# Two tokens to a partition in the first two steps of a gated linear-attention and FFN kernel: batches of a pair in separate halves of the partitions

## Chip, cores and metric

The kernel runs on one core of one Trainium2 chip. The metric is the device time of one execution in microseconds (us). A core has a matrix engine (PE, with a separate row PEld for its weight loads), a vector engine (DVE), an activation engine (ACT), a general engine (POOL), a sync engine (SP) that issues DMAs, and 16 DMA engines that all queues share. PE reads its operands from SBUF (128 partitions) and writes into PSUM (8 banks of 128 partitions by 512 float32).

## What is computed

A recurrence over 768 tokens for 4 batches and 8 heads of width 48, and a feed-forward network on its output:

```python
f = 1.0 / (1.0 + np.exp(-f_logit))
for t in range(S):
    state = f[:, :, t, :, None] * state + np.einsum('bhd,bhe->bhde', k[:, :, t], v[:, :, t])
    y[:, :, t] = np.einsum('bhd,bhde->bhe', q[:, :, t], state)
x = np.ascontiguousarray(attn_out.transpose(0, 2, 1, 3)).reshape(B * S, H * D)
gate = np.maximum(x @ w_gate, 0.0)
out = gate * (x @ w_val) @ w_out          # 3072 x 384 -> 1536 -> 384
```

Inputs and output are float32 in HBM. A token's 48 values of one head are 192 contiguous bytes, and two neighbouring tokens of a head are 384.

## The kernel before

**Steps.** The tokens are cut into six steps (c = 0 to 5) of 128 tokens. A step has four batches, worked on as two pairs (0, 1) and (2, 3). For each pair the kernel loads f, k, q, v (384 KB each, one DMA each). Then, per batch: ACT turns f into log-gates (exp, then ln), PE sums them along the tokens with a triangular matrix, ACT takes the exponentials of plus and minus that sum, and products give scaled k and q ("hats"). They are transposed so that head columns lie on partitions (into qkT). Scores k.q within the step are matmuls of 48 rows, two head parities in two row tiles of the PE array; DVE multiplies them by a causal mask (ptm). "intra" (L759) makes the transposed output y in four column tiles of 128 rows by 32 columns from ptm and v (vpad), and from step 1 on from the state of the step before too; ACT copies y to xT. "state" (L810) makes the new state's sum from hats and vpad.

**Steps 0 to 2 and 3 to 5.** In steps 1 and 2 the hats are transposed on PE (`pe_hats`), from step 3 on by DMA. Step 0 is special (`twos = (0,)`): for f, k and q a partition holds two neighbouring tokens, so that DMA packets are 384 bytes instead of 192; the partition is 2 x (token pair) + (batch of the pair), so that even and odd partitions belong to different batches. Two masks (`upto`, `below`) that keep the batches apart do the summing over tokens, with two matmuls of 384 columns for each of the two tokens i. After the transposes a token order with one batch to a row is restored by strides (`tokens`). v of step 0 is loaded with one token to a partition. The state needs k with one token to a partition too, so `attention_back` (L631 to L637) transposes the hats of k back on PE, four matmuls and one DVE copy for each batch, behind the outputs of step 0.

**FFN.** For each hidden block j of 12, three matmuls for the gate and three for the value (L834; 512 columns, or 256 where half of the batches are taken alone: blocks 0 to 5 of steps 0 to 2, `halves`), a ReLU on ACT (L840), a product on DVE (L844); then 12 matmuls of 384 columns for each batch (L877), a copy on ACT and a store. The last batch of all is split in two (L857).

**Order of the work.** A planner (`Plan`) takes every operation with a cost and a priority, simulates five engine queues, the DMA queue and eight PSUM banks with a limit for each kind of tile, and fixes one order for each engine; waits on semaphores are derived from it. FFN operations have a low priority on PE (P + 1000) and fill what attention leaves. On the chip each engine works through its list in that order, whatever is late.

**Loads.** SP issues f0.0 k0.0 q0.0 v0.0 f0.1 k0.1 q0.1 v0.1 (step.pair), later f1.0 and so on. POOL issues the nine weight loads, which also turn float32 to bfloat16, in thirds: wg0 only after f0.1 has landed, wv0, then wg1 only after q0.1, wv1, wg2, wv2, and wo0 after q1.0. f1.0 is issued only after wv1 has landed. The list is `first` (L319). Until 15 us the plan puts matmuls on zeros (L938) between PE's real work.

Of the kernel before, what the change touches and what calls it, by code (L numbers as in the profile page):

```python
# [299 lines left out]
def bass_hgrn2_outer__then__ffn_reglu_kernel(  # L300
# [10 lines left out]
    twos = (0,)  # L311
    pe_hats = {(1, 0), (1, 1), (2, 0), (2, 1)}
    halves = {0: 6, 1: 6, 2: 6}
    x_way = {(c, pr): "tiled" if c < 3 else "xbar" for c in range(6) for pr in range(2)}
    s_twin = {(c, pr) for c in range(6) for pr in range(2)} - {(0, 0), (1, 0)}
    y_twin = {(1, 1), (2, 0), (2, 1)}
# [57 lines left out]
    pick2 = sb("pick2", [128, 2], BF16)  # L374
    ident = sb("ident", [128, 128], BF16)
# [4 lines left out]
    pl = Plan({"bc": 2, "bc4": 4, "tp": 2, "s": 4, "y": 2, "kv": 1, "f": 4})  # L380
# [28 lines left out]
    def triangle(t, name, base, prio):  # L409
# [9 lines left out]
                                         pattern=[[0, 64], [1, 2]], channel_multiplier=-1), ["pick"], ["pick"], occ=0.3, prio=-20)  # L419
# [10 lines left out]
    add("DVE", lambda: ve.tensor_copy(pick2[:], same.ap[:, 0:2]), [same], ["pick2"], occ=0.1, prio=-19)  # L430
# [30 lines left out]
    def load(n, c, b0, b1, after=()):  # L461
        last = tails.get("load")
        t = ld[n]
        both = c in twos and n != "v"
        if both:
            src = bass.AP(tensor=srcs[n].tensor, offset=b0 * H * S * D + c * C * D,
                          ap=[[2 * D, C // 2], [S * D, 2 * H], [1, 2 * D]])
            dst = bass.AP(tensor=t, offset=slot_of(n, c, b0 // 2) * 2 * HD, ap=[[NL[n] * 2 * HD, 128], [2 * D, H], [1, 2 * D]])
        else:
            src = bass.AP(tensor=srcs[n].tensor, offset=b0 * H * S * D + c * C * D,  # L470
                          ap=[[D, C], [S * D, (b1 - b0) * H], [1, D]])
            dst = t[:, slot_of(n, c, b0 // 2), :, :, :].rearrange("p b h d -> p (b h) d")
        op = add("SP", lambda: sy.dma_start(dst, src), [], in_keys(n, c, b0, b1),  # L473
                 occ=0.7 if both else 1.0, lat=0.9, prio=c * 100, after=after,
                 follows=[last] if last else [])
        tails["load"] = op
        dma(op, f"{n}{slot_of(n, c, b0 // 2)}", 0.95 * (b1 - b0), (64, 19, 27) if both else (128, 13.5, 23))
        return op
# [20 lines left out]
    loads, done = [], {}  # L499
    for item in first:  # L500
        item, _, behind = item.partition("@")
        gate = [done[behind]] if behind else []
        if item[0] == "w":
            op = load_w(item[:2], int(item[2:]), gate)
        else:
            c, pr = (int(x) for x in item[1:].split("."))
            op = load(item[0], c, 2 * pr, 2 * pr + 2, gate)
        done[item] = op
        if item[0] != "w":
            loads.append(op)  # L510

    def chain(line, *args, **kw):

        last = tails.get(line)
        tails[line] = add(*args, follows=[last] if last else [], **kw)
        return tails[line]
# [10 lines left out]
    def tokens(c, b, x, p, lo=0, hi=128):  # L527
        qi = (c * B + b) % NQ
        if c not in twos:
            return qkT[lo:hi, qi, x, p, :]  # L530
        row, two = NQ * 2 * NP * C, b % 2
        return bass.AP(tensor=qkT, offset=lo * row + (qi - two) * 2 * NP * C + x * 2 * NP * C + p * 2 * C + two,
                       ap=[[row, hi - lo], [2, C]])
# [18 lines left out]
    def attention_pair(c, b0):  # L552
# [3 lines left out]
        raw = {n: ld[n][:, slot_of(n, c, pr), :, :, :].rearrange("p b h d -> p (b h d)") for n in "fkq"}  # L556
        by_i = {n: raw[n].rearrange("p (h i d) -> p i h d", h=H, i=2) for n in "fkq"}
        key = {n: in_keys(n, c, b0, b0 + 2) for n in "fkq"}
# [6 lines left out]
            follows=tails.pop("first q", []), **act_t(2 * HD))  # L565
        heads = lambda b_: b_.ap[:, 0:HD].rearrange("p (h d) -> p h d", h=H)
        for i in range(2):
            bc, ek = Bank("bc4"), Bank("bc4")

            def cum(i=i, bc=bc):  # L570
                for o in range(2):
# [3 lines left out]
            ex = expo[:, e0 + i, 0, :]  # L575
            add("ACT", lambda bc=bc, ek=ek: sc.activation(ek.ap[:, 0:HD], bc.ap[:, 0:HD], AF.Exp, scale=1.0),
                [bc], [ek], prio=P + 2 + i, opens=[ek], **act_t(HD))
            eqk = bc if i else f"expq{e0}_0"
            add("ACT", lambda bc=bc, i=i, ex=ex: sc.activation(bc.ap[:, 0:HD] if i else ex, bc.ap[:, 0:HD], AF.Exp, scale=-1.0),
                [bc], [eqk], prio=P + 2 + i, **act_t(HD))  # L580
            e, hi = ("DVE" if i else "POOL"), his[i]
            hk_op = add("DVE", lambda i=i, hi=hi, ek=ek: ve.tensor_tensor(hats[:, hi, 1, :, 0:D], by_i["k"][:, i], heads(ek), ALU.mult),
                        key["k"] + [ek, f"hats{hi}"], hk_(hi), prio=P + 2 + i, **dve_t(HD))
            add(e, lambda e=e, i=i, hi=hi, bc=bc, ex=ex: engine[e].tensor_tensor(
                hats[:, hi, 0, :, 0:D], by_i["q"][:, i], heads(bc) if i else ex.rearrange("p (h d) -> p h d", h=H), ALU.mult),
                key["q"] + [eqk, f"hats{hi}"], hq_(hi), prio=P + 3 + i, follows=[hk_op] if i else [], **elem_t(e, HD))
# [9 lines left out]
        for j in range(2):  # L596
            lo = 64 * j
            add("ACT", lambda lo=lo, j=j: sc.activation(
                dec[ai][lo:lo + 64, b0:b0 + 2, :, j].rearrange("p b n -> p n b"),
                tot.ap[lo:lo + 64, 0:2 * NP].rearrange("p (n b) -> p n b", n=NP), AF.Exp, scale=-1.0),  # L600
                [tot, f"dec{ai}"], [f"dec{ai}_{b}{j}{hh}" for b in (b0, b0 + 1) for hh in range(2)], prio=P + 10, **act_t(8))
        for x in (1, 0):
            tp = Bank("tp")

            def transposes(x=x, tp=tp):
                t16 = tp.ap[:, :].bitcast(BF16)
                for p in range(NP):
                    for i in range(2):
                        mm = te.transpose(t16[:, 2 * C * p:2 * C * (p + 1)].rearrange("q (r i b) -> q r i b", i=2, b=2)[:, :, i, :],
# [5 lines left out]
            e = "DVE" if x else "ACT"  # L615
            op = add(e, (lambda tp=tp, dst=dst: sc.activation(dst, tp.ap[:, :].bitcast(BF16), AF.Copy)) if e == "ACT"  # L616
# [3 lines left out]
            if not x and b0 == 0:  # L620
                tails["first q"] = [op]

    def attention_back(c, b, behind):
        w = c * B + b
        hi, qi = w % NH, w % NQ
        tp = Bank("tp")

        def transposes():
            t16 = tp.ap[:, :].bitcast(BF16)
            for p in range(NP):  # L630
                mm = te.transpose(t16[:, p * C:(p + 1) * C], tokens(c, b, 1, p), ident[:])  # L631
            return mm
        P = w * 10
        tails["transposes"] = add("PE", transposes, ["ident", f"qkT{qi}_10", f"qkT{qi}_11"], [tp], occ=0.3, lat=PE_L, prio=P + 30,
                                  opens=[tp], follows=[behind, tails["transposes"]])
        add("DVE", lambda: ve.tensor_copy(hats[:, hi, 1, :, :].rearrange("p h d -> p (h d)"), tp.ap[:, :].bitcast(BF16)[:, 0:4 * C]),
            [tp], hk_(hi), prio=P + 31, follows=[behind], **dve_t(256))  # L637

    def attention_front(c, b):
# [32 lines left out]
        if c < NC - 1:  # L672
            for j in range(2):
# [9 lines left out]
        add("POOL", lambda: gp.tensor_tensor(hq, qin[:, b % 2, :, :], ex[:, 0, :].rearrange("p (h d) -> p h d", h=H),  # L683
                                             ALU.mult),
            in_keys("q", c, b, b + 1) + [f"expq{ei // 2 * 2}_{ei % 2}", f"hats{hi}"], hq_(hi), prio=P + 2, **pool_t(HD))
# [21 lines left out]
    def attention(c, bs):  # L707
        units = []
        for b in bs:
# [5 lines left out]
                in_keys("v", c, b, b + 1) + [f"vpad{w % NV}"], [f"v_{w % NV}"], prio=w * 10 + (55 if c in twos else 3), **pool_c(HD))  # L715
# [58 lines left out]
        xi, ybank, yop = c % NX, {}, {}  # L774
        tiled = x_way[c, bs[0] // 2] == "tiled"
        for part in ([units] if tiled and (c, bs[0] // 2) in y_twin else [[u] for u in units]):
# [4 lines left out]
            op = chain("intra", "PE", rows, [t for u in part for t in need(u) + ([f"vpad{u[1] % NV}"] if tiled else [])], ys,  # L781
                       occ=(0.34 if c else 0.19) * len(part) + 0.235 if tiled else 0.38, lat=PE_L, prio=part[0][1] * 10 + 7, opens=ys)
            for u, y in zip(part, ys):
                ybank[u[0]], yop[u[0]] = y, op
        for b, w, _ in units:
# [12 lines left out]
            if c in twos:  # L798
                behind.append(yop[b])
                later.append(lambda b=b, w=w: update(c, b, w))  # L800
            elif c < NC - 1:
                update(c, b, w)

    def update(c, b, w):
# [9 lines left out]
        if c in twos:  # L814
            attention_back(c, b, behind[-1])
        chain("state", "PE", state, hk_(hi) + [f"hats{hi}", f"v_{w % NV}"], [kv],
              occ=0.18, lat=PE_L, prio=P + (32 if c in twos else 6), opens=[kv])
        new_state(kv, c, b, w, P + (25 if c in twos else 0))
# [50 lines left out]
    def ffn_out(g, bs, cuts=1):  # L869
# [14 lines left out]
        for b in bs:  # L884
# [5 lines left out]
            both = [(bass.AP(tensor=out.tensor, offset=at, ap=[[DM, C], [1, DM]]), osb[oi][:, :])]  # L890
# [4 lines left out]
    groups = {c: [(0, 2, range(0, n)), (2, 4, range(0, n)), (0, 4, range(n, NJ))] for c, n in halves.items()}  # L895
    pend = []
    for c in range(NC):
# [4 lines left out]
        behind, later = [], []  # L902
        for b in range(0, B, 2):
# [5 lines left out]
            attention(c, (b, b + 1))  # L909
# [24 lines left out]
    order = pl.settle([(bk, warm_until if bk is spare else 0.0) for bk in banks], rounds=8, early=set(done.values()))  # L934
# [94 lines left out]
```

## Time and profile before

| what | value |
|---|---|
| median of three runs (lowest, highest) | 196.01 us (194.18, 196.87) |
| the profiled execution | 195.26 us |
| its span from first to last instruction | 193.5 us |
| PE busy | 184.2 us, 95% |
| ACT, DVE, POOL busy | 111.0, 106.1, 75.9 us |
| granted PE clock | 1.00 |
| DMA packets, data | 118,196; 31.74 MB |
| of them under 512 bytes | 111,136 |
| queue of SP, share of 16 engines' time | 68.1% |
| queue of POOL (weights) | 11.4% |

A time in the tables of the profile is in us from the start of the span. A group of instructions is written by line, engine, operation and tile, with its count, its busy time and the mean of one. "idle before" is the time in which the engine stood still ahead of these instructions, with what released it. The PE's matmuls are pipelined and their recorded ends are modelled, so this document takes the distance from one start to the next as the cost of a matmul group, and not the recorded durations.

### The profile page before, as it was taken

How to read it: one execution, taken by the hardware profiler on the slowest of the kernel's cores; microseconds unless marked ns; L12 is line 12 of the kernel's file. 1: busy time of each engine (PE TensorE's matmuls, PEld its weight loads, DVE VectorE, ACT ScalarE, POOL GpSimd, SP SyncE). 2: the span in 40 equal slices, each digit the busy share in tenths (PEclk: the TensorE clock that was granted, in tenths of full speed). 3: DMA queues.
4: the chain of work that ended last, by engine and by line, in shares of the span. 5: the costliest groups of instructions: out<-in, count | busy, mean ns of one | idle time of the engine just before them, and what ended most of it. 6: DMA issues, size and time to landing. Idle time of an engine off the chain costs nothing.

```text
span 193.5 us, 4448 instructions
## 1 busy us (share of the span) xinstructions
PE 184.2 (95%) x1773; PEld 110.7 (57%) x1790; DVE 106.1 (55%) x195; ACT 111.0 (57%) x250; POOL 75.9 (39%) x108
## 2 busy tenths in 40 slices
PE   6986898999999999999999999999999999999995
PEld 1445694465788556767755544554555555544564
DVE  7756884671668878354776643743635622443300
ACT  3777439763596779838757758377343544244322
POOL 8377002958275949783533471634230000000000
PEclk9999999999999999999999999999999999999999
DMA  4999999999898999999796998998954220111113
GB/s 131 276 283 207 206 201 207 207 199 239 199 244 167 202 201 192 231 193 247 161 192 132 194 207 172 221 226 170 204 87 106 64 61 0 41 41 44 41 43 119
DMA packets 118196, 31.74 MB, mean 164 GB/s; under 512 B 111136, under 2 KB 118176, under 8 KB 118176
## 3 DMA queue, kind: packets, MB, share of 16 engines
q1 hardware_dynamic: 114192, 27.93, 68.1%
q0 software_dynamic: 3984, 3.54, 11.4%
q8 instruction: 14, 0.23, 0.5%
q14 instruction: 6, 0.05, 0.1%
HBM read 25.95 MB, written 4.72 MB: 158 GB/s over the span
## 4 chain that ended last, share of the span: by engine, by line
PE 70%; DMA 16%; SPq 5%; ACT 2%; DVE 2%; POOL 2%; issue 1%
PE ps L834 36%; PE ps L877 23%; DMA q_in<-in_q_dram 6%; DMA wv<-in_moe_w_val_dram 5%; SPq L473 4%; DMA f_in<-in_f_logit_dram 3%; DMA v_in<-in_v_dram 3%; PE ps L724 2%; PE ps L658 2%; PE ps L694 2%; PE ps L759 1%; PE ps L810 1%; DVE ptm L734 1%; PE ps L857 1%; POOL hats L683 1%
## 5 line engine op out<-in xcount | busy, mean ns | idle before, releaser
L844 DVE TENSOR_TENSOR gT<-relu,ps 128x512 bf16<-128x512 bf16 (+1 forms) x90 | 51.2, 578 | 53.9 <-PE ps L834 38.8
L834 PE MATMUL ps<-xT,wv 128*128 128x512 bf16 (+1 forms) x263 | 60.2, 336 | 1.8 <-DMA wv<-in_moe_w_val_dram 1.3
L840 ACT ACTIVATE relu<-ps 128x512 bf16<-128x512 f32 (+1 forms) x90 | 45.3, 511 | 27.6 <-PE ps L834 27.0
L834 PE MATMUL ps<-xT,wg 128*128 128x512 bf16 (+1 forms) x261 | 59.6, 335 | 0.9 <-ACT relu L840 0.5
L877 PE MATMUL ps<-wo,gT 128*128 128x384 bf16 x276 | 49.5, 326 | 0.1
L877 PEld LDWEIGHTS ps<-wo,gT 128*128 128x128 bf16 x276 | 25.9, 98 | 17.2
L834 PEld LDWEIGHTS ps<-xT,wv 128*128 128x128 bf16 x270 | 24.6, 98 | 19.4 <-DMA wv<-in_moe_w_val_dram 1.7
L834 PEld LDWEIGHTS ps<-xT,wg 128*128 128x128 bf16 x270 | 25.2, 98 | 17.9 <-ACT relu L840 0.4
L734 DVE TENSOR_TENSOR ptm<-ps,tri 128x512 bf16<-128x512 f32 x48 | 30.5, 684 | 8.3 <-PE ps L724 8.2
L680 POOL TENSOR_TENSOR hats<-k_in,expo 128x384 bf16<-128x384 f32 x20 | 19.8, 1000 | 20.8 <-ACT expo L668 11.0
L887 ACT ACTIVATE osb<-ps 128x384 f32<-128x384 f32 x23 | 11.2, 489 | 26.1 <-PE ps L877 26.1
L683 POOL TENSOR_TENSOR hats<-q_in,expo 128x384 bf16<-128x384 f32 x20 | 19.8, 1000 | 6.5 <-DMA q_in<-in_q_dram 6.5
L549 POOL TENSOR_TENSOR st<-ssum,dec 128x384 bf16<-128x384 f32 x16 | 13.3, 830 | 15.7 <-DVE ssum L547 15.5
L649 ACT ACTIVATE f_in<-f_in 128x768 f32<-128x768 f32 x10 | 8.4, 843 | 12.1 <-DMA f_in<-in_f_logit_dram 12.1
L714 POOL CAST vpad<-v_in 128x384 bf16<-128x384 f32 x24 | 11.7, 505 | 3.2 <-DMA v_in<-in_v_dram 3.2
L547 DVE TENSOR_TENSOR ssum<-ps,st 128x384 f32<-128x384 f32 x16 | 8.8, 552 | 4.9 <-PE ps L810 4.9
L668 ACT ACTIVATE expo<-ps 128x384 f32<-128x384 f32 x20 | 9.9, 493 | 0.5 <-PE ps L661 0.3
L670 ACT ACTIVATE expo<-ps 128x384 f32<-128x384 f32 x20 | 9.9, 496 | 0.0
L699 DVE COPY qkT<-ps 128x1024 bf16<-128x1024 bf16 x8 | 5.5, 690 | 7.5 <-PE ps L694 7.4
L724 PEld LDWEIGHTS ps<-qkT 48*128 48x128 bf16 x192 | 5.4, 94 | 5.3 <-issue 1.9
L651 ACT ACTIVATE bneg<-f_in 128x768 bf16<-128x768 f32 x10 | 8.4, 836 | 0.0
L724 PE MATMUL ps<-qkT 48*128 48x128 bf16 x192 | 7.6, 217 | 0.6 <-ACT qkT L616 0.5
(76 smaller groups left out, 146.2 us busy)
## 6 DMA issues: line engine op xcount, KB each, us to landing
f_in<-in_f_logit_dram SPq DMA_DIRECT2D x12, 384.0 KB, 5.6
k_in<-in_k_dram SPq DMA_DIRECT2D x12, 384.0 KB, 4.9
q_in<-in_q_dram SPq DMA_DIRECT2D x12, 384.0 KB, 5.7
v_in<-in_v_dram SPq DMA_DIRECT2D x12, 384.0 KB, 5.3
out_dram<-osb SPq DMA_DIRECT2D x23, 192.0 KB, 2.4
wg<-in_moe_w_gate_dram POOLq DMA_DIRECT2D x3, 384.0 KB, 7.7
wv<-in_moe_w_val_dram POOLq DMA_DIRECT2D x3, 384.0 KB, 8.8
wo<-in_moe_w_out_dram POOLq DMA_DIRECT2D x3, 384.0 KB, 6.2
```

The lines of the kernel that those rows point to most:

```text
L549: add("POOL", lambda: gp.tensor_tensor(t4(s_new), t4(tmp), rate, ALU.mult), [key] + dk, [f"S{b}_{c % 2}"], prio=P + 8, **pool_t(HD))
L668: add("ACT", lambda: sc.activation(ex[:, 1, :], bc.ap[:, 0:HD], AF.Exp, scale=1.0), [bc], [f"expk{ei}"], prio=P + 1, **act_t(HD))
L680: add("POOL", lambda: gp.tensor_tensor(hk, kin[:, b % 2, :, :], ex[:, 1, :].rearrange("p (h d) -> p h d", h=H), ALU.mult), in_keys("k", c, ...
L683: add("POOL", lambda: gp.tensor_tensor(hq, qin[:, b % 2, :, :], ex[:, 0, :].rearrange("p (h d) -> p h d", h=H), ALU.mult), in_keys("q", c, ...
L714: add("POOL", lambda vin=vin, vout=vout: gp.tensor_copy(vout, vin.rearrange("p (n j) d -> p n j d", j=2)), in_keys("v", c, b, b + 1) + [f" ...
L724: mm = te.matmul(s[j].ap[:, p * C:(p + 1) * C], tokens(c, b, 1, p, lo, lo + D), tokens(c, b, 0, p, lo, lo + D))
L734: add("DVE", lambda mi=mi, j=j, s=s: ve.tensor_tensor(ptm[mi][:, j, :, :], s.ap[:, :].rearrange("p (n t) -> p n t", n=NP), mask, ALU.mult) ...
L834: mm = te.matmul(bank.ap[:, 0:n], wt[:, kt, j * 128:(j + 1) * 128], xT[xi][:, kt, n0:n1], start=(kt == 0), stop=(kt == NK - 1))
L840: add("ACT", lambda: sc.activation(relu[ri][:, 0:n], gate.ap[:, 0:n], AF.Relu), [gate], [f"relu{ri}"], prio=P, **act_t(n))
L844: add("DVE", lambda: ve.tensor_tensor(gT[gi][:, j, n0:n1], relu[ri][:, 0:n], val.ap[:, 0:n], ALU.mult), [val, f"relu{ri}"], [f"gT{gi}_{j}_ ...
L877: mm = te.matmul(o[b].ap[:, 0:DM], gT[gi][:, j, b * C:(b + 1) * C], wo[:, j, :], start=(j == 0), stop=(j == NJ - 1))
L887: add("ACT", lambda b=b, oi=oi: sc.activation(osb[oi][:, :], o[b].ap[:, 0:DM], AF.Copy), [o[b]], [f"osb{oi}"], prio=P, **act_t(DM))
```

## The change

Steps 0 and 1 (`twos = (0, 1)`) now both work on pairs with two tokens to a partition. The partition is 64 x (batch of the pair) + (token pair): each batch has 64 partitions of its own. v is loaded in the same way. Each of these sixteen loads is now two DMAs, one for each half of the partitions. Transposes need no strides. Scores are matmuls of 48 rows by 64 columns in 64x64 tiles (32 for a pair instead of 16), masked with a new mask `mask2` for each of the two tokens i. Outputs from ptm and v are matmuls in 64x32 tiles (64 for a pair instead of 32), one chain for both batches; in step 1 the part from the old state stays in 128x32 tiles (24 for a pair). States are matmuls in 64x128 tiles, two that add up for each batch and pair of heads (16 for a pair instead of 8). `attention_back` is gone. In step 1 the sums over tokens take two matmuls of 384 columns for each token i, as in step 0, and the scaled q of its first pair are made on DVE instead of POOL. In step 0 the copy of the transposed q moves from ACT to DVE. The PSUM limit of "kv" goes from 1 to 2. The rows of the output stores of steps 0 and 1 are permuted in the address pattern of the store.

```diff
-    twos = (0,)
-    pe_hats = {(1, 0), (1, 1), (2, 0), (2, 1)}
+    twos = (0, 1)
+    pe_hats = {(2, 0), (2, 1)}
...
+    on_dve = {(1, 0, 0, 0), (1, 0, 0, 1)}
...
-    pl = Plan({"bc": 2, "bc4": 4, "tp": 2, "s": 4, "y": 2, "kv": 1, "f": 4})
+    pl = Plan({"bc": 2, "bc4": 4, "tp": 2, "s": 4, "y": 2, "kv": 2, "f": 4})
...
+    for i, src, name in ((0, upto, "upto"), (1, below, "below"), (1, upto, "upto")):
+        lo = [m for m in range(2) if not (i and (name == "upto") != (m == 1))]
+        add("POOL", lambda i=i, src=src, lo=lo: gp.tensor_tensor(
+            mask2[:, i, lo[0]:lo[-1] + 1, :], src[:, 0:64].unsqueeze(1).to_broadcast([128, len(lo), 64]),
+            src[:, 64:128].unsqueeze(1).to_broadcast([128, len(lo), 64]), ALU.add), [name], [f"mask2_{i}{m}" for m in lo],
+            prio=-9, **pool_t(64 * len(lo)))
...
-        both = c in twos and n != "v"
+        both, one = c in twos, b1 - b0 == 1
         if both:
-            src = bass.AP(tensor=srcs[n].tensor, offset=b0 * H * S * D + c * C * D,
-                          ap=[[2 * D, C // 2], [S * D, 2 * H], [1, 2 * D]])
-            dst = bass.AP(tensor=t, offset=slot_of(n, c, b0 // 2) * 2 * HD, ap=[[NL[n] * 2 * HD, 128], [2 * D, H], [1, 2 * D]])
+            row = NL[n] * 2 * HD
+            moves = [(bass.AP(tensor=t, offset=64 * i * row + slot_of(n, c, b0 // 2) * 2 * HD, ap=[[row, 64], [2 * D, H], [1, 2 * D]]),
+                      bass.AP(tensor=srcs[n].tensor, offset=(b0 + i) * H * S * D + c * C * D,
+                              ap=[[2 * D, C // 2], [S * D, H], [1, 2 * D]])) for i in range(2)]
...
-    def attention_back(c, b, behind):
...
+        def scores(its):
+            for i in its:
+                for p in range(NP):
+                    for j in range(2):
+                        for b in range(2):
+                            mm = te.matmul(s[i][j].ap[64 * b:64 * b + 64, p * C:(p + 1) * C],
+                                           tokens(c, b0 + b, 1, p, 64 * j, 64 * j + D, i), tokens(c, b0 + b, 0, p, 64 * j, 64 * j + D))
...
+            for i in range(2):
+                for at, (n, p, col, j) in enumerate(todo):
+                    lo = 32 * (n % 4)
+                    for b in range(2):
+                        mm = te.matmul(y[b].ap[lo:lo + 32, n // 4 * C:(n // 4 + 1) * C],
+                                       vpad[vs[i]][64 * b:64 * b + 64, col:col + 32], ptm[ms[i]][64 * b:64 * b + 64, j, p, :],
+                                       start=(first and i == 0 and at < 4), stop=(i == 1 and at >= 12), skip_group_check=True)
...
+            def state():
+                for p in range(NP):
+                    for i in range(2):
+                        for b in range(2):
+                            mm = te.matmul(kv[b].ap[:, p * 96:(p + 1) * 96],
+                                           hats[64 * b:64 * b + 64, his[i], 1, 2 * p:2 * p + 2, :].rearrange("p h d -> p (h d)"),
+                                           bass.AP(tensor=vpad[vs[i]], offset=64 * b * VW + p * VSTEP, ap=[[VW, 64], [64, 2], [1, D]]),
+                                           start=(i == 0), stop=(i == 1), skip_group_check=True)
```

## The prediction

> **What bounds the kernel now.** I read the page first: PE is busy 95%. The PE timeline says since when. The first FFN matmul is at 16.58; two waits on weights follow and one on ACT, and from 31 to 66 us PE stands still for no more than 0.2 us at a time:
>
> ```profile
> 16.58 0.49 PE L834 MATMUL ps<-xT,wg 128*128 128x256 bf16 x3
> ...
> 18.12 0.50 PE L834 MATMUL ps<-xT,wv 128*128 128x256 bf16 x3 [0.60 <-DMA wv<-in_moe_w_val_dram]
> ...
> 22.67 0.50 PE L834 MATMUL ps<-xT,wv 128*128 128x256 bf16 x3 [0.71 <-DMA wv<-in_moe_w_val_dram]
> ...
> 30.27 0.60 PE L834 MATMUL ps<-xT,wg 128*128 128x512 bf16 x2 [0.50 <-ACT relu L840]
> ```
>
> The number after the start is the length; brackets give the idle time and its releaser. The third wait is a ReLU behind the exp of f1.0, which waits for its load at the head of ACT's queue. Later gaps come to 2 us in all. So the end is: arrival of the weights, plus PE's work after it. The POOL timeline shows what sets the weights:
>
> ```profile
> 10.68 0.96 POOL L493 DMA_DIRECT2D wg<-in_moe_w_gate_dram  x1 [0.79 <-DMA f_in<-in_f_logit_dram]
> 11.63 0.78 POOL L493 DMA_DIRECT2D wv<-in_moe_w_val_dram  x1
> 13.06 0.77 POOL L493 DMA_DIRECT2D wg<-in_moe_w_gate_dram  x1 [0.64 <-DMA q_in<-in_q_dram]
> ```
>
> The weights wait for f0.1 and q0.1, and these for what lies ahead in SP's queue. The page's second part shows the DMA engines full from there on, with two rates:
>
> ```profile
> DMA  4999999999898999999796998998954220111113
> GB/s 131 276 283 207 206 201 207 207 199 239 199 244 167 202 201 192 231 193 247 161 192 132 194 207 172 221 226 170 204 87 106 64 61 0 41 41 44 41 43 119
> ```
>
> A slice is 4.84 us: loads run at some 280 GB/s, weights alone at 206. Counted in the trace's packets: 864 packets of 384 bytes in the best microsecond (18.5 ns each on one of 16 engines), 1,335 of 192 bytes (12.0 ns). A load of 384 KB is thus 64 packets an engine, 1.2 us, or 128 packets, 1.5 us. First packet at 2.34; f0.1 has landed at 10.03, q0.1 at 12.46, wg0 15.86, wv0 17.77, wv1 22.30, a third every 1.9 us.
>
> **What the Trainium skill says.** "SBUF — State Buffer", Door 1: The DMA port swizzle: 64 partitions reach only 8 of the 16 ports, 196 GB/s measured for 1 MiB against 328 with 128 partitions, and two DMAs to the two halves ran only 6% faster than one. The kernel before has no such load, so nothing here shows it; its loads span all partitions at 280. "DMA: Bandwidth & Descriptors", Queues, rings and completion order: engines switch between queues by packets of several descriptors. The trace agrees that weights hold SP's queue back: from 35 to 36 us 198 weight packets went and 27 of SP's, though SP had loads queued. "TensorEngine Tiling (Array Packing)", Key Properties: tiles work side by side, a change of mode drains the array. The trace agrees: sixteen scores take 51.43 to 51.99 = 0.56, where two tiles side by side give 16 x 28.3 ns = 0.45, so 0.1 for the drains.
>
> **PE's work, part by part.** From the timeline, start to start:
>
> ```profile
> 55.86 0.35 PE L759 MATMUL ps<-qkT,st 128*32 128x128 bf16 x12
> 56.04 0.40 PE L759 MATMUL ps<-ptm,vpad 128*32 128x128 bf16 x16
> 56.26 0.34 PE L759 MATMUL ps<-qkT,st 128*32 128x128 bf16 x12
> 56.43 0.40 PE L759 MATMUL ps<-ptm,vpad 128*32 128x128 bf16 x16
> 56.76 0.50 PE L834 MATMUL ps<-xT,wv 128*128 128x256 bf16 x3
> ```
>
> 56 matmuls in 0.90: 14.2 ns each (four tiles, 56.6 ns per 128 columns) and 0.1.
>
> Step 1 before: sums 0.53 a pair (38.98 to 39.51), scores 0.56 and 2 x 0.33, outputs 0.90 and 2 x 0.51, states 4 x 0.17. Together 1.06 + 1.22 + 1.92 + 0.68 = 4.9 us; transposes are the same before and after. After, a pair: sums 4 x 0.165 (L572, 12.94 to 13.60) + totals 0.20 (eight L592, 7.17 to 7.37) = 0.86; scores 32 in four tiles, 32 x 14.2 ns + 0.1 = 0.55; outputs 24 x 14.2 ns + 64 x 7.1 ns + 0.15 = 0.95 if eight tiles overlap; states 16 of 96 columns (42.5 ns alone, two side by side), between 0.34 and 0.68 plus 0.1, I take 0.5. Twice that: 5.7. Step 1 costs +0.8.
>
> Step 0 after the wait at 22.67: `attention_back` goes, 0.68 + 0.22 (L631) = -0.9; states +0.3. Scores and outputs of its second pair lie ahead of that wait and are covered (+0.1 if not). Sum for PE: +0.2. Bounds: that eight tiles issue fast enough is not shown; the trace has weight load and matmul of one tile starting 3.5 ns after those of the last, eight make 28 ns, within 56.6, so I take the overlap. If only four overlapped: +0.45 for each pair of step 1, +0.9.
>
> **The ramp.** Each load becomes two DMAs. SP's issue of one load takes 0.65 to 0.74 (1.61 and 0.81 in its timeline), the shortest issue of any 0.33; two halves of 0.4 stay below a load's transfer. v0.0 and v0.1 get 384-byte packets. If ports don't matter: 1.2 instead of 1.5, twice; f0.1 lands 0.3 to 0.5 earlier. If each half is held to 8 ports: an engine writes 384 bytes in 18.5 ns; by the 218 GB/s that the skill states for 8 ports (an estimate from "SBUF — State Buffer", Door 1) it is 384 x 16 / 218 = 28.2 ns, 1.8 us a load. Between lies this: the sixteen landings of one load in the trace are spread over 0.34 to 0.5 us and half a load lasts 0.6, so engines that share a port are partly out of step. I take 25 ns, 1.6 us. Then f0.1 has landed at 2.34 + 5 x 1.6 + 0.35 = 10.7 (+0.65), q0.1 at 13.9 (+1.4), still ahead of the first weight data (13.5 + 0.65 = 14.2), so wg1 follows without a hole. v0.1 now ends beside the weights and costs them some 0.5. wv1: +1.1, and PE with it.
>
> Of the rest ahead of the weights: the q copy leaves ACT (1.0 us at 11.15, in front of ln f0.1) for DVE at about 10.65, so the first scores come 0.8 earlier than 12.21; outputs then wait for all four masks, not two, and xT is ready at 16.2, as now (16.25). Covered by wv0; without that cover it would be worth 0.3 either way. The v casts on POOL (8.94) stand ahead of wg0's issue; v0.0 lands at 9.1, casts end by 10.1, before f0.1. mask2's three small POOL operations fall into its idle time from 4.6 to 8.0. Off PE the rest moves work that is not the bound: DVE loses four copies of 0.42 and gains two products of 0.55 and the two copies of 0.69; POOL loses two products of 1.0.
>
> **New waits in step 1.** Transposes, scores, outputs and states now wait for a whole pair. In the kernel before, the outputs of step 1's second pair come at 55.86 and its xT is used from about 57.4, little slack; q1.1 lands at 46.09. Step 1's loads take 1.6 instead of 1.5, no gain. The head-of-queue wait at 30.27 moves along with wv1. I put 0.3 on this, from -0.7 (that wait gone) to +1.5.
>
> **Sum.** 1.1 (weights) + 0.2 (PE) + 0.3 = +1.6 us: the profiled execution 195.26 (span 193.5 and 1.8 around it) becomes 196.9; the median of the runs shown stands 0.75 above it, 197.6.
>
> **Rivals.** (1) Ports don't matter. For: the halves alternate in one queue, and 384-byte packets are bound by the engine when alone. Then weights -0.5 and PE and waits +0.2: 195.7. (2) The halves run in step at 28.2 ns, and q0.1 falls behind the weights. f0.1 lands at 11.8, weight data starts at 15.3, q0.1's data would end at 15.0 and its landing at 15.4: a little later and the weights hold it back until wg0 and wv0 are through, 19.1. Then POOL issues wg1 at 19.4, 2.9 us later (10.68 to about 13.5 now) data comes, wv1 lands at 26.3 instead of 22.3: +4.0, with PE's +0.2 and the waits' 0.3: 200.5, slower. It decides from about 28 ns a packet. For it: the measurement on that page; against it: the spread of landings. (3) Eight tiles don't overlap, and the pair's chains stall PE beside the late weights: 1.6 + 0.9 = +2.5, 198.5.
>
> **Chances and range.** Likeliest case 0.40, its own range 196.6 to 198.8; rival 1 0.22; rival 2 0.30; rival 3 0.08. Range 194.6 (rival 1 with its waits at -0.7 and its run a little low) to 200.9 (rival 2). A measurement of this kernel can tell about 2% from no change, 192.1 to 199.9. Slower: 0.24 of rival 2 and 0.07 of the others' upper ends; faster: 0.05, rival 1 with all early waits gone.
>
> **What will show it.** Time from first to last packet of the eight first loads: 9.8 us (rival 1), 12.8 (mine), 14.4 (rival 2). POOL's first weight issue at 10.3, 11.3 or 12.4, the second gated one after q0.1 at about 14.5 or 19. PE's L834 wait on wv at 23.8. The 64 small output matmuls of a pair in 0.55 us, or 1.0 if four overlap. I am wrong if a long PE gap stands in step 1 (35 to 62 us), or if the weights are on time and the time is not.

## The result, and the profile after

The changed kernel takes 225.16 us (224.46 to 225.33, four runs) against 196.44 us (194.18 to 197.11, four runs): 1.150 times as long, interval 1.139 to 1.160. Some executions are over 1.5% slower than the fastest of the same kernel, and the ratios leave them out. The forecast was 197.6, with a range to 200.9. What it missed is nowhere in the prediction's sum: the address pattern of the output stores, which leaves two DMA engines to carry each of them.

The span of the profiled execution grew from 193.5 to 223.5 us, by 30.0. PE's busy time grew from 184.2 to 192.9 us and its idle time from 9.3 to 30.6. So 21 us are waits. The other 9 us are mostly the same work at a lower clock: the mean granted clock was 0.947 instead of 1.00, and in a later run of the same matmuls at full clock ("all DMAs as before" below) PE was busy 182.8 us. The page's second part says where. A slice is 5.59 us here:

```profile
PE   7865989999994089999277499999999999999995
...
PEclk9998599999999769999969859999999999999999
DMA  5999999999546299994673969599896110100012
GB/s 130 240 234 205 208 236 192 240 193 195 129 107 136 63 222 202 215 192 100 64 147 78 142 142 219 127 204 241 114 196 144 55 54 35 38 35 31 17 61 106
```

PE falls to 4 and 0 in the 13th and 14th slice (67 to 78 us) and to 2, 7, 7 and 4 in the 20th to 23rd (106 to 128 us). The DMA engines, full up to the tenth slice, are at 6 and 2 tenths in the first of these stretches, with 63 GB/s in its second slice, and at 4, 6, 7 and 3 from the 19th to the 22nd. PE is short of data while DMA engines stand idle. The PE timeline names two of the long waits:

```profile
79.05 0.50 PE L896 MATMUL ps<-vpad,hats 128*128 128x96 bf16 x4 [7.31 <-POOL vpad L803]
...
113.39 1.03 PE L813 MATMUL ps<-qkT 48*128 48x128 bf16 x16 [5.78 <-DMA qkT<-hats]
```

The first waits for the copy of v2.1 (step 2, second pair) on POOL. The chain of waits shows that copy's reason (start, length, what); its next two lines here lead to two further PE waits, until 121.10 and until 127.27:

```profile
67.77 10.66 DMA v_in<-in_v_dram
...
112.61 7.61 DMA v_in<-in_v_dram
120.22 7.00 DMA qkT<-hats
```

The load of v2.1 takes 10.66 us. What stands right ahead of it is in SP's timeline, which shows issues, not transfers:

```profile
65.37 2.35 SPq L976 DMA_DIRECT2D out_dram<-osb  x2
67.77 1.44 SPq L485 DMA_DIRECT2D v_in<-in_v_dram  x1
69.25 7.54 SPq L485 DMA_DIRECT2D f_in<-in_f_logit_dram  x1
...
100.53 5.74 SPq L976 DMA_DIRECT2D out_dram<-osb  x1
106.32 1.97 SPq L791 DMA_TRANSPOSE qkT<-hats  x1
```

Two output stores go out, then the load of v, and the next load is stuck in its issue for 7.54 us. The second long wait has a store ahead of it too: the transposes that PE waits for until 113.39 are issued at 106.32, behind a store whose issue took 5.74 us. Counted in the trace's packets (a store is 128 packets of 1,536 bytes), the stores of steps 0 and 1 take 4.3 to 5.5 us each and 8.4 for the two together, with 2.1 packets in flight at a time; the later ones, with plain rows, take 0.63 to 0.81 us with 12 to 15 in flight. The median packet takes 65 ns in both. Before the change a store alone took 0.6 to 1.4 us.

The change writes these eight stores as `[[DM, 2], [2 * DM, 64], [1, DM]]`. The Trainium skill, "DMA: Bandwidth & Descriptors", section "Why a DMA increments its semaphore by 16 and not by 1", states that the number of engines of a DMA is the largest up to 16 that divides the slowest dimension of both patterns. Here that is 2, and the trace agrees with its 2.1 packets in flight.

The ramp is late as well. POOL's weight issues, which answer to those at 10.68 and 13.06, and the PE timeline:

```profile
12.61 0.94 POOL L506 DMA_DIRECT2D wg<-in_moe_w_gate_dram  x1 [0.99 <-DMA f_in<-in_f_logit_dram]
...
15.89 0.78 POOL L506 DMA_DIRECT2D wg<-in_moe_w_gate_dram  x1 [1.57 <-DMA q_in<-in_q_dram]
```

```profile
19.82 0.49 PE L918 MATMUL ps<-xT,wg 128*128 128x256 bf16 x3
21.65 0.82 PE L918 MATMUL ps<-xT,wv 128*128 128x256 bf16 x3 [1.34 <-DMA wv<-in_moe_w_val_dram]
...
34.86 0.59 PE L918 MATMUL ps<-xT,wg 128*128 128x512 bf16 x2
```

The group of 512 columns, which stood at 30.27, is a good mark for the end of the ramp: 4.6 us late. The matmuls at 0.82 instead of 0.49 us run at half clock, which the trace shows from 20.8 to 27.7 us.

### The profile page after: what moved, and what is told of

Its sections match the earlier page's. It is cut to its first block, busy times and chain, and to the rows that moved or that the text cites. A ratio compares the mean times of both kernels' runs of the same rounds, so it can differ in the third digit from the quotient of the medians.

```text
span 223.5 us, 4889 instructions
## 1 busy us (share of the span) xinstructions
PE 192.9 (86%) x1981; PEld 115.6 (52%) x1999; DVE 108.7 (49%) x195; ACT 109.0 (49%) x244; POOL 75.0 (34%) x109
## 4 chain that ended last, share of the span: by engine, by line
PE 72%; DMA 17%; SPq 6%; ACT 2%; issue 1%; POOL 1%
PE ps L918 40%; PE ps L961 19%; DMA v_in<-in_v_dram 8%; DMA wv<-in_moe_w_val_dram 4%; DMA qkT<-hats 3%; SPq L485 3%; DMA f_in<-in_f_logit_dram 2%; PE ps L813 2%; SPq L884 2%; PE ps L747 1%; PE ps L691 1%; PE ps L658 1%; PE ps L896 1%; PE ps L941 1%; PE ps L860 1%
## 5 line engine op out<-in xcount | busy, mean ns | idle before, releaser
L918 PE MATMUL ps<-xT,wv 128*128 128x512 bf16 (+1 forms) x264 | 63.9, 351 | 1.9 <-DMA wv<-in_moe_w_val_dram 1.3
L918 PE MATMUL ps<-xT,wg 128*128 128x512 bf16 (+1 forms) x259 | 62.6, 351 | 1.6 <-ACT xT L704 0.7
L823 DVE TENSOR_TENSOR ptm<-ps,tri 128x512 bf16<-128x512 f32 x32 | 20.5, 684 | 17.6 <-PE ps L813 17.6
L769 POOL TENSOR_TENSOR hats<-k_in,expo 128x384 bf16<-128x384 f32 x16 | 15.9, 999 | 31.8 <-ACT expo L757 29.0
L773 POOL TENSOR_TENSOR hats<-q_in,expo 128x384 bf16<-128x384 f32 x16 | 15.9, 1000 | 8.9 <-DMA q_in<-in_q_dram 8.9
L567 POOL TENSOR_TENSOR st<-ssum,dec 128x384 bf16<-128x384 f32 x16 | 13.1, 830 | 10.2 <-DVE ssum L565 10.2
L803 POOL CAST vpad<-v_in 128x384 bf16<-128x384 f32 x16 | 7.9, 508 | 17.5 <-DMA v_in<-in_v_dram 17.5
L565 DVE TENSOR_TENSOR ssum<-ps,st 128x384 f32<-128x384 f32 x16 | 8.5, 551 | 10.8 <-PE ps L896 10.2
L896 PE MATMUL ps<-vpad,hats 128*128 128x96 bf16 x48 | 4.2, 212 | 8.6 <-POOL vpad L803 8.6
L667 DVE TENSOR_TENSOR ptm<-ps,mask 128x512 bf16<-128x512 f32 x16 | 9.9, 682 | 1.1 <-PE ps L658 1.0
L757 ACT ACTIVATE expo<-ps 128x384 f32<-128x384 f32 x16 | 7.8, 490 | 2.3 <-PE ps L750 1.3
L882 ACT ACTIVATE xn<-ps 128x384 bf16<-128x384 f32 x12 | 5.9, 489 | 6.1 <-PE ps L860 6.0
```

The lines of the kernel that those rows point to most:

```text
L565: add("DVE", lambda: ve.tensor_tensor(tmp[:, :], kv.ap[:, 0:HD], s_old[:, :], ALU.add), [kv, f"S{b}_{(c + 1) % 2}"], [key], prio=P + 8, ** ...
L567: add("POOL", lambda: gp.tensor_tensor(t4(s_new), t4(tmp), rate, ALU.mult), [key] + dk, [f"S{b}_{c % 2}"], prio=P + 8, **pool_t(HD))
L667: add("DVE", lambda i=i, j=j, mask=mask: ve.tensor_tensor(ptm[ms[i]][:, j, :, :], s[i][j].ap[:, :].rearrange("p (n t) -> p n t", n=NP), ma ...
L769: add("POOL", lambda: gp.tensor_tensor(hk, kin[:, b % 2, :, :], ex[:, 1, :].rearrange("p (h d) -> p h d", h=H), ALU.mult), in_keys("k", c, ...
L773: add(e, lambda: engine[e].tensor_tensor(hq, qin[:, b % 2, :, :], ex[:, 0, :].rearrange("p (h d) -> p h d", h=H), ALU.mult), in_keys("q", ...
L823: add("DVE", lambda mi=mi, j=j, s=s: ve.tensor_tensor(ptm[mi][:, j, :, :], s.ap[:, :].rearrange("p (n t) -> p n t", n=NP), mask, ALU.mult) ...
```

## The experiments

Theory A: the stores' pattern puts each store on two DMA engines, and loads queued behind them come late. Theory B: the loss is in the engines' work or in new waits of the pairs. Theory C: the halved loads carry a loss of their own in the ramp.

**Stores in two halves.** In the changed kernel:

```diff
-            both = [(... ap=([[DM, 2], [2 * DM, 64]] if g in twos else [[DM, C]]) + [[1, DM]]), osb[oi][:, :])]
+            both = ([(... offset=at + i * DM, ap=[[2 * DM, 64], [1, DM]]), osb[oi][64 * i:64 * i + 64, :]) for i in range(2)]
+                    if g in twos else [...])
```

> The changed kernel with one edit: each output store of steps 0 and 1 is issued as two stores of 64 rows, the same addresses, so that the outermost dimension of a store is 64 instead of 2. Theory A (the store's address pattern puts 128 packets on two DMA engines, 4.3 us a store instead of 0.6, and loads queued behind it on these two engines come late): the PE gaps at 67 to 80 us and at 102 to 130 us close, some 20 to 23 us go, and 199 to 205 us stay; what is left over the kernel before is the late start (21.65 instead of 18.12 us) and the slow PE clock around it. Rival B (the pairwise chains of the new layout run attention late, and the slow stores only fill a queue that nobody waits for): at most 5 us go, 220 or more.

203.89 us (202.09 to 204.98), 1.045 of before (1.036 to 1.053). Stride and rows are the same; the outermost count changed from 2 to 64, in two DMAs of 64 partitions each. 21 us are gone, and a store (both halves) now lasts 1.05 to 1.3 us in most cases. Its packets take about 107 ns at the median, not 65.

**The pattern alone, in the kernel before.** One line, for steps 0 and 1 (these output rows are out of order):

```diff
-            both = [(... ap=[[DM, C], [1, DM]]), osb[oi][:, :])]
+            both = [(... ap=([[DM, 2], [2 * DM, 64]] if g in (0, 1) else [[DM, C]]) + [[1, DM]]), osb[oi][:, :])]
```

> The kernel before with one edit: the output stores of steps 0 and 1 take the changed kernel's address pattern, so that 8 of the 24 blocks of output rows come out permuted. Layout, loads and matmuls stay those of before. Theory A (two DMA engines carry each of these stores): 211 to 222 us, with PE gaps after about 60 us behind late loads. Rival B (the cost lies in the new layout): 195 to 198 us.

222.65 us (221.71 to 223.59), 1.139 of before (1.126 to 1.151). With nothing else of the change the pattern costs 26 us, a little over the upper end expected. Its PE timeline has the same signature, among others a wait for the copy of a late v:

```profile
62.14 1.04 PE L694 MATMUL ps<-ident,hats 128*128 128x128 bf16 x8 [3.97 <-POOL hats L683]
...
125.14 0.50 PE L810 MATMUL ps<-vpad,hats 128*128 128x96 bf16 x4 [10.00 <-POOL vpad L714]
```

Its ramp is that of before (the 512-column mark at 30.00), so all 26 us come later than that.

**Four and eight engines.** If the count is what matters, the loss must follow it.

```diff
-ap=([[DM, 2], [2 * DM, 64]] if g in twos
+ap=([[DM, 4], [4 * DM, 32]] if g in twos        # the other: [[DM, 8], [8 * DM, 16]]
```

> The changed kernel with one number of the stores' pattern changed: the rows of steps 0 and 1 go out as 4 groups of 32 rows instead of 2 groups of 64 (left out: these rows are out of order). Theory A (the outermost count of the pattern is the number of DMA engines that carry the store): 64 packets a us, 2.0 to 2.7 us a store instead of 4.2 to 5.5, and 204 to 213 us. The rival (the pattern is slow for its stride or for its broken rows): still over 4 us a store and 220 to 227 us.

> As the run before, with 8 groups of 16 rows (left out: these rows are out of order). Theory A: 1.0 to 1.6 us a store, 199 to 203 us, close to the 199.7 of plain rows. The rival: still over 4 us a store and 220 to 227 us.

213.87 us (210.89 to 214.22), 1.087 of before (1.076 to 1.098), and 202.90 us (202.81 to 202.95), 1.036 (1.030 to 1.043). The first time lies just above the range expected, the second inside its own. A single store lasts 2.9 to 3.9 us with 3.1 to 3.8 packets in flight, then 1.4 to 2.4 us with 5 to 7, the median packet still 65 ns. Both are longer than expected; that other traffic shares the engines is a guess. The load of v behind the stores shrinks alongside: 10.66 us above, and in the chains of these two

```profile
63.59 7.41 DMA v_in<-in_v_dram
```

```profile
63.55 5.34 DMA v_in<-in_v_dram
```

The outermost count, and with it the number of packets in flight, is settled as the cause; a stride of several rows is not it.

**Loads in one DMA, and loads in two over all partitions.** With the half-stores, each load of steps 0 and 1 as one DMA over 128 partitions, or as two of half the bytes that each cover all partitions (the batches of a pair are mixed in the partitions in both):

```diff
-moves = [(... offset=64 * i * row + ..., ap=[[row, 64], [2 * D, H], [1, 2 * D]]), ...) for i in range(2)]
+moves = [(... ap=[[row, 128], [2 * D, H], [1, 2 * D]]), ...)]
...
+moves = [(... offset=... + i * HD, ap=[[row, 128], [2 * D, H // 2], [1, 2 * D]]), ...) for i in range(2)]
```

> The stores in halves as in the first kernel of this set, and each load of f, k, q, v of steps 0 and 1 as one DMA over all 128 partitions with the same packets of 384 bytes; partitions then hold tokens of mixed batches, so the output is not the reference's, and the work is the same. Theory C (two DMAs of 64 partitions are what makes the start late): the first FFN value matmul comes at 17.5 to 18.3 us instead of 21.65, no slow PE clock follows, and the time is 4 to 6 us below the first kernel of this set, 195 to 198. Rival D (the start is late for the attention chain of the pair, masks and outputs, or for the fillers on PE): less than 1.5 us below it.

> As the third kernel of this set, but each load is again two DMAs, each over all 128 partitions with half of the bytes (output mixed in the same way). If the 8 ports of half the partitions are the cost, it runs like the third (within 1.5 us of it) with packets at about 18.5 ns an engine; if the doubled number of DMA instructions on SP is the cost (1.3 us of issue for each load instead of 0.7), it runs like the first, with f of the second pair landing near 12 us.

The loads in one took 199.21 and 202.75 us, of which only the first is compared: 4.7 below the run with half-stores, as theory C had it, though above 198. The first value matmul came at 17.18, earlier than expected. The loads in two over all partitions took 206.22 us (205.47 and 206.98; 1.055 of before, 1.044 to 1.066). POOL's first weight issue separates the two costs of a halved load: 9.86 in one DMA, 11.11 in two over all partitions, 12.31 in halves of the partitions. So in these traces about half of the delay is the second DMA, half the half partitions. The whole time does not show the second part: two DMAs over all partitions are no faster than halves (206.22 and 203.89, with ratios whose intervals overlap). Why stays open.

The chain of the run with loads in one shows what else was left. The half-stores (L977) stand in front of a load of v and of DMA transposes on SP's queue:

```profile
59.63 0.60 SPq L977
60.27 3.90 DMA v_in<-in_v_dram
...
96.77 0.59 SPq L977
97.41 0.61 SPq L977
98.06 3.32 DMA qkT<-hats
```

**The order made in the copy, and all DMAs as before.** The copy of the outputs to xT puts the tokens in order, so that a store is one DMA of plain rows (L975). The second kernel has plain stores too, without that copy, and the loads in one DMA. In the first:

```diff
-            dst = xT[xi][:, :, (b0 + b) * C:(b0 + b + 1) * C]
-            src = lambda b=b: y[b].ap[:, 0:HD].rearrange("p (n t) -> p n t", n=NK)
+            dst = xT[xi][:, :, (b0 + b) * C:(b0 + b + 1) * C].rearrange("p n (t i) -> p n i t", i=2)
+            src = lambda b=b: y[b].ap[:, 0:HD].rearrange("p (n i t) -> p n i t", n=NK, i=2)
...
+            both = [(bass.AP(tensor=out.tensor, offset=at, ap=[[DM, C], [1, DM]]), osb[oi][:, :])]
```

> The changed kernel, but the copy of the outputs of steps 0 and 1 from PSUM to xT writes column 64 i + t to column 2 t + i, so that the feed-forward rows are in token order again and each store is one DMA of plain rows (as before the change); the loads stay in halves. Theory D (in the run with half-stores, 203.9 us, the eight extra store DMAs on SP's queue, 0.6 us each, held up load v2.1 and what follows it): 199.5 to 201.5 us, stores of 0.6 to 1.1 us, and v2.1 no longer behind two pairs of stores. Theory E (the half-stores were free, and what is left over the kernel before, 7.7 us, is the halved loads and PE's work): 203 to 205 us. If the copy's stride of two columns is dear, ACT's copies show more than the 0.5 us or so of before and the time is above 205.

> Every load and every store of steps 0 and 1 is one DMA over 128 partitions with plain rows, as in the kernel before (left out: the two batches of a pair are mixed in the partitions and the rows of the outputs are out of order); the work on the engines is that of the changed kernel. Theory D (the DMA side carries nearly all of the loss: two-engine stores, doubled DMAs on SP, halved loads): 195.5 to 198.5 us, and the predicted +0.2 for PE's work and +0.3 for new waits fit in it. The rival (the work on the engines or the new waits of step 1 cost some us themselves): 200 to 203 us, about what the loads in one with half-stores took (201.0).

199.67 us (199.36 to 199.86), 1.020 of before (1.017 to 1.023), and 194.84 us (193.78 to 198.42, twelve runs), 0.999 of before (0.995 to 1.002); before ran at 195.10 beside them. The second is the answer to theory B: with the DMAs as before, the changed work on the engines costs nothing and gains nothing that the time shows (its ramp is 0.7 us earlier, the mark at 29.58, so a cost of that size could hide). The difference of the two puts a price of 4.8 us on the halved loads, with the copy's stride in it. The copies show the stride: the view of the line has, for the changed kernel and then for this one (minimum, median, maximum in ns),

```profile
L704 ACT ACTIVATE xT<-ps x8: 484/488/491, 17.2 to 58.2; 128x384 bf16<-128x384 f32 x8
```

```profile
L704 ACT ACTIVATE xT<-ps x8: 579/598/606, 16.4 to 57.4; 128x384 bf16<-128x384 f32 x8
```

110 ns eight times, on an engine with idle time.

These two kernels and the two with half-stores make a square of two loads by two stores:

| | halved loads | loads in one |
|---|---|---|
| half-stores | 203.89 | 199.21 |
| plain stores | 199.67 | 194.84 |

Halving the loads costs 4.7 us in one row and 4.8 in the other. The half-stores cost 4.2 in one column and 4.4 in the other; before was 1.1 us slower beside the upper row (196.17 and 195.10), so 3 to 4 us, about what theory D gave them. With the loads in one the ramps are alike (marks at 29.47 and 29.58) and the spans still differ by 4.6, so there the cost comes later. In the traces with halved loads the spans differ by only 2.3, and 1.7 of that is there before any store goes out (marks at 33.63 and 31.92), so that pair of traces alone would not show it.

In the kernel with the order made in the copy the loss of 4.5 us in the span against before lies in three places: the mark at 31.92 instead of 30.27 (1.7); from 36 to 48 us PE busy 10.16 instead of 11.84 (1.7); from 100 to 140 us 38.07 instead of 39.17 (1.1). The second is two waits of whole pairs for the scaled q and k:

```profile
38.16 1.07 PE L633 MATMUL ps<-ident,hats 128*128 128x128 bf16 x16 [0.83 <-POOL hats L606]
...
47.30 0.62 PE L633 MATMUL ps<-ident,hats 128*128 128x128 bf16 x8 [0.80 <-POOL hats L606]
```

Its chain leads back from there to the q load:

```profile
35.25 9.97 DMA q_in<-in_q_dram
45.22 0.07 issue
45.29 1.96 POOL hats L606 x2
47.25 0.05 issue
47.30 0.62 PE ps L633 x8
```

With the loads in one, POOL starts the last scaled q of step 1 at 42.96 instead of 47.20, and PE is busy 11.79 of these 12 us. In the kernel before, POOL gets the same q only at 46.09 and PE has no such wait. So it takes both: loads this late, and work that waits for a whole pair.

**Step 0 alone, fillers, earlier gates.** Three edits to the kernel with the order made in the copy: step 1 put back; the fillers on PE allowed for longer; the weights' gates moved up, without and with the first load of step 1.

```diff
-    twos = (0, 1)
+    twos = (0,)                    # and pe_hats, s_twin, y_twin, on_dve of step 1 as before
...
-    warm_until = 15.0
+    warm_until = 24.0
...
-    first = (... wg0@f0.1 wv0 wg1@q0.1 ... f1.0@wv1
+    first = (... wg0@v0.0 wv0 wg1@k0.1 ... f1.0@wv1       # the last run: f1.0@wv0
```

> The kernel with the order made in the copy, and step 1 put back to its former way (128 tokens of one batch on the partitions, loads in one DMA): only step 0 is changed. If the price is in the ramp (f0.1 and the other step-0 halves late, weights late behind them), it stays: 199 to 201 us, within 1.5 us of the same kernel with both steps changed. If the halves of step 1's loads carry it (they stand between the ramp's loads and the weights), this one is 2 to 4 us shorter than that: 196 to 198 us.

> The kernel with the order made in the copy, with the fillers on PE allowed until 24 us of the planner's time instead of 15, so that PE is not idle while it waits for the late first weights. If the half clock at about 20 to 27 us (6.8 us in the changed kernel) is a price of its own, the clock stays 1.0 there and the time falls by 1.5 to 3 us under the same kernel without them. If the late loads alone set the time, it stays within 0.7 us; if the fillers get in the way, it rises.

> The kernel with the order made in the copy (199.7 us), with the first two gates of the weights' issues moved up by three and two loads: wg0 behind v0.0 instead of f0.1, wg1 behind k0.1 instead of q0.1, so that the weights start about as early as before the change (wg0 at 9 to 10.5 us instead of 12.2). If the late weights are the price of the halves, the first value matmul comes at 18 to 19.5 us and the time is 196.5 to 198.5. If the step-1 halves on SP's queue (10.8 us of issue, then q1.1 until 45.2 us in the chain) set it, the time stays at 199 to 201. The planner draws its order anew here, which moves some work on every engine.

> The kernel with earlier gates for the weights, and the first load of step 1 behind the second weight third (wv0) instead of the fourth (wv1), so that SP starts its 16 half-loads of step 1 earlier, if it stood in the chain with 24.4 to 35.3 us. If that queue carries what is left of the loss: 194.5 to 197.5 us and q1.1 landed before 43 us. If the loads only take bandwidth from the weights: 198 to 202 us, with the first value matmul 1 to 3 us later than in the run with the gates alone.

Step 0 alone: 198.37 us (197.62 to 200.45), 1.015 of before (1.009 to 1.022). This lies between the two outcomes expected. Most of the 4.8 us thus seems to come with step 0's halves, in the ramp (first weight issue at 12.28, as with both steps); step 1's add about 1.3, less than the 2.8 us by which these four runs scatter.

Fillers: 200.30 us (199.84 to 201.54), 1.025 (1.020 to 1.030), no gain. The half clock now lay between 14 and 18 us, no FFN group ran at it, and the mark stood at 32.01 against 31.92. The kernel without the longer fillers had three such groups, so these three cost nothing there and the late weights set the mark.

Gates: 201.72 us (201.42 to 205.88) and 202.10 us (201.75 to 203.85), 1.030 and 1.035: a little above what the theory of step 1's queue expected of the first, and just above the range of the second theory for the other, whose first value matmul came only 0.3 us later (21.64 after 21.34), not 1 to 3. Neither theory is shown by it. The weight issue moved to 10.30 as meant, but POOL then issues weights ahead of the copy of v, and PE's first outputs of the second pair wait for that:

```profile
17.28 1.06 PE L691 MATMUL ps<-ptm,vpad 64*32 64x128 bf16 x64 [2.83 <-POOL vpad L648]
...
20.70 0.85 PE L918 MATMUL ps<-xT,wg 128*128 128x256 bf16 x3
```

The first gate matmul is at 20.70 instead of 19.79. In this order of work the weights were not free to go earlier; the planner drew its order anew, so another order is not ruled out. No version here beats the kernel before.

## Why the prediction was wrong

**The step that failed is the sum itself:** "1.1 (weights) + 0.2 (PE) + 0.3 = +1.6 us". It has no term for the output stores. The prediction does not name them at all; its part on the ramp follows only the DMAs of the loads. That the rows of the stores are permuted in their address pattern stands in the section on the change, and was taken to cost nothing. The missing term measures +26 us alone in the kernel before, and 25.5 as the difference of the changed kernel to the one with plain stores (225.16 and 199.67), 2.9 of which are there before any store goes out. It could have been had from what was at hand: 128 packets of 65 ns on two engines are 4.2 us a store, eight stores, all in a queue that feeds every later load. No rival held it, so no range could. The prediction took a page of the skill on partitions for the loads and did not hold the stores to the rule on the slowest dimension told above.

How a store of 4 to 5 us comes to hold up PE is in part argued. A load behind it in the queue is spread over more engines, so I take it to end when the busy ones get to it. The traces do not name the engine of a packet; the 10.66, 7.41 and 5.34 us of the same load behind stores with counts of 2, 4 and 8 speak for it (in the kernel before, the median load of v took 5.3).

The other steps, one by one:

- "I take 25 ns, 1.6 us": the trace has about 625 packets a microsecond over 16 engines, 25.6 ns, so the size held, between the two rivals' values. That is 240 GB/s, above the 196 that the prediction quotes for 64 partitions, and by more than the 6% that it quotes for two halves (a figure that stands further on in that page, under "Can I just issue two DMAs to hit both halves?"). With 128 partitions in one DMA it is about 845 packets, or 324 GB/s. With two DMAs over all partitions it is 735 to 784, so the half partitions are only part of the difference.
- "f0.1 has landed at 10.7 (+0.65)": too early. Five loads' bytes had gone by 10.77, but the exp that needs f0.1 began at 12.33 instead of 10.40, +1.9. What was mis-sized is the time from a load's share of the bytes to its last piece: 0.7 us before, 1.6 with halves. POOL's weight issue came at 12.61, by the forecast's own test in the class of rival 2 (12.4), yet wg1 followed at 15.89 without that rival's hole (19.4). The eight first loads took 14.2 us from first to last packet, rival 2's sign again (14.4), but the last of them shared the engines with weights from 15.4 on.
- "two halves of 0.4 stay below a load's transfer": a half costs SP 0.65, as much as a whole load before. The pair of 1.31 to 1.57 us takes nearly all of the 1.6 us of transfer; the doubled DMA alone put the weights 1.25 us later (9.86 to 11.11).
- "wv1: +1.1, and PE with it": +4.6 at the 512-column mark, +1.7 in the kernel with plain stores. The two have the same loads and no store before the mark. The difference goes with the clock: at half clock ran eight of the 24 FFN groups of 256 columns in the changed kernel, three in the other. In three other kernels with halves and eight such groups the mark was at 33.6 to 34.3, in one with five at 33.17, and in one with none at 32.01. The two kernels with earlier gates don't fit this row (35.15 and 35.37 with two and four); their order of work differs. The Trainium skill, "TensorE: Matmul & The Clock Gate", section "What's actually happening", states that an idle window of about 3.4 us halves the clock and that windows run freely; the stretches at half clock within these kernels last 3.4, 6.8 or 10.2 us. That the clock costs these 2 to 3 us is inferred; no run isolates it, and the one with longer fillers had only three such groups to remove and gained nothing.
- "Sum for PE: +0.2": not contradicted. With all DMAs as before the ratio is 0.999 (0.995 to 1.002), and 0.2 us is too small to be told from nothing. The overlap of eight tiles held, against rival 3:

```profile
49.37 0.52 PE L681 MATMUL ps<-qkT,st 128*32 128x128 bf16 x24
49.82 0.73 PE L691 MATMUL ps<-ptm,vpad 64*32 64x128 bf16 x64
50.49 0.62 PE L633 MATMUL ps<-ident,hats 128*128 128x128 bf16 x8
...
52.14 0.64 PE L658 MATMUL ps<-qkT 48*64 48x128 bf16 x32
52.71 0.50 PE L961 MATMUL ps<-wo,gT 128*128 128x384 bf16 x2
```

  Start to start, 64 outputs take 0.67 us (0.55 forecast, 1.0 if four overlapped) and 32 scores 0.57 (0.55).
- "I put 0.3 on this, from -0.7 to +1.5": no long gap from 35 to 62 us in the changed kernel, whose ramp was later. In the kernel with plain stores the waits of whole pairs on POOL are 1.6 us (0.83 and 0.80). With loads in one they are absent, so they need the halves as well as the pairs.

With plain stores the forecast of +1.6 us would have met +4.6, inside the range, but with its terms wrong: the ramp's +1.1 should have been +1.7, the waits' 0.3 should have been 1.6, and 1.1 lies in the stretch from 100 to 140 us, for which there was no term.

## What to carry to other kernels

Read the pattern of every DMA that a change touches, stores too: here its outermost count set how many engines carried it, and a store that nobody waits for still held up the loads queued behind it. A permutation of rows is better made where an engine writes through SBUF anyway (110 ns a copy here) than in a store's outer dimension. A DMA split in two paid its issue twice here, and two halves of the partitions did not move as fast as one DMA over all; a change that wins nothing on the engines can't carry that.

## What the runs showed of the hardware

- The median packet of 1,536 bytes took 65 ns with an outermost count of 2, 4 or 8, and with plain rows mostly too (up to 99 ns); what changed was the number in flight (2.1, 3.1 to 3.8, 5 to 7, up to 13 or more), and the time of a store with it (4.3 to 5.5, 2.9 to 3.9, 1.4 to 2.4, from 0.63 us).
- In the stores issued as two halves of 64 partitions most stores had a median packet of about 107 ns, in all three kernels that have them.
- SP's issue of a DMA of half the bytes took 0.65 us in the ramp, the shortest of a whole one there as well.
- Packets of 384 bytes: 845 a microsecond with 128 partitions in one DMA, 735 to 784 with two DMAs over all partitions, 625 with two of 64 partitions each.
- An ACT copy of 128x384 from PSUM to bf16 with a stride of two columns took 598 ns at the median instead of 488.
